# Feature sums of a linear attention: added up in one tile, formed behind the denominators, turned a period later

## The chip, the cores and the metric

The kernel runs on one core of one Trainium2 chip. A core has a matrix engine (TensorE, PE in the profile; its weight loads are PEld), a vector engine (DVE), an activation engine (ACT), a general one (POOL) and a queue that issues DMAs (SP). The metric is the device time of the whole program in microseconds, the median of several runs; less is better.

## The reference

Linear attention over 8 batches and 8 heads of 576 positions, followed by a dense layer pair.

```python
def phi(x):
    proj = np.einsum('bhsd,df->bhsf', x, w_phi)
    proj = proj - np.max(np.abs(proj), axis=-1, keepdims=True)
    return np.concatenate([np.exp(proj), np.exp(-proj)], axis=-1)
q_p, k_p = (phi(q), phi(k))
kv = np.einsum('bhsf,bhsd->bhfd', k_p, v)
z = np.sum(k_p, axis=2)
num = np.einsum('bhsf,bhfd->bhsd', q_p, kv)
den = np.einsum('bhsf,bhf->bhs', q_p, z)[..., None] + 1e-06
attn = num / den            # heads side by side: x, 4608 x 512
h = x @ w_in                # 512 -> 2048
out = (h - np.tanh(h)) @ w_out
```

z are the feature sums: 256 per head (128 features, two signs).

## The kernel before

**Stage one, attention.** A unit is a pair of heads (e = 0, 1) of one batch; there are NU = 32 of them, and u.i is a unit's number. A unit's 576 positions of q and of k make 9 blocks of 128: four and a half of q, four and a half of k. The half block of k is tile j = 0 of five (64 rows, from SR = 64 up), the whole ones are j = 1 to 4.

The work is a pipeline over periods, period(i) for i from 0 to 32, written out by hand: inside manual_schedule every engine's queue follows the order of the program. In period i the unit a = i is projected, c = i - 1 gets its products of k and v and the exponentials of q, p = i - 2 its numerators and denominators, r = i - 3 its reciprocals, and q = i - 4 the multiplication by them and its store. Beside that, a weight block w per period is decoded on DVE from 64-bit numbers (dec_0 on ACT, dec_1 to dec_3 on DVE), and in periods 3 to 16 one is split into a high and a low part (split_w).

PE's order in a period, with the names of its outputs in the profile:

- project(a, 0): pp, three blocks of both heads. DVE then takes the largest magnitude (L223) and subtracts it (less_max, L230) into tile t. The PSUM tile of pp has one buffer, so each project waits for the subtraction of the one before.
- num(p): po, the numerators, from kv and the exponentials qe of q.
- project(a, 1), then kv(c): pc, the products of k's features with v. ACT copies it to kvt (kv_copy, L291).
- project(a, 2).
- ksum(c): pk, the feature sums as products with a column of ones. The full tiles 1 to 4 were added up by POOL before (kadd, L274 to L276: three adds into the tile t of the third projection), so pk takes that sum and then the half tile apart. ACT copies pk to kst (ksum_copy).
- q_side(c): ptr and ptt, transposes of q's blocks; ACT takes their exponentials.
- turn(c): ptk, transposes of the two halves of kvt and of kst; DVE copies them to SBUF (turn_copy, L305).
- denom(p): pd, the denominators; ACT copies them to dd (denom_copy), and SP loads them into another layout (dn, den_recip_load).

A period later DVE takes the reciprocals (rn, L357 and L358), SP sends them through DRAM (rr) to all partitions (rb), and after that POOL multiplies (den_mul, L367) and SP stores the result to xs. All these DMAs stand in the one queue of SP in program order, with the loads of q, k, v and the raw weights.

POOL's helper behind(x) copies one column of a tile (mark, L186), which makes POOL wait until DVE has written it; it stands ahead of POOL's part of split_w (L96) and at a period's end behind the decode.

On PE, one fp32 matmul stands as two records in the profile. A shape such as 128*32 is the rows and columns of the array that a matmul takes: pk with the full tile and pd both have 128*32, pk with the half tile has 64*32, pp and ptr 64*128, ptt and ptk 128*128, po and pc 128*64.

**Stage two, the dense layers.** The result is read back in groups of 384 tokens: x_load brings four column blocks (192 KB each), x_split makes a high part on ACT (L114) and a low one on DVE (L115). The tile x has four buffers. The four blocks of the first group are loaded at the start of period 30 and split at the end of period 31. Stage two (L508 on) then runs 192 steps, a step being one group by one block of 128 hidden features; its order is left to the planner, but for the instructions marked with pin.

What follows the periods (L490 to L496) is also left to the planner: the reciprocals, multiplications and stores of the last three units.

Of the kernel before, what the change touches and what calls it, by code (L numbers as in the profile page):

```python
# [8 lines left out]
F32 = mybir.dt.float32  # L9
# [4 lines left out]
ALU = mybir.AluOpType  # L14
# [5 lines left out]
P = 128  # L20
# [12 lines left out]
def tile_linear_attention_moe(  # L33
# [10 lines left out]
    nc = tc.nc  # L44
    B, H, S, D = dims
    F = w_phi.shape[1]
# [4 lines left out]
    SR = S - SM  # L51
# [4 lines left out]
    G = 3  # L56
    AHEAD = 7
    PC = 2 * S
    NCT = DM // P
# [8 lines left out]
    ident = consts.tile([P, P], F32, name="ident")  # L68
# [10 lines left out]
    xp0 = ctx.enter_context(tc.tile_pool(name="xp0", bufs=1, reuse_waits="tile"))  # L79
# [25 lines left out]

    def x_load(g, xt, c):
        bp, o = divmod(g * G, TPP)
        x = xp0.tile([P, G * P], F32, tag="x", name=f"x{g}_{c}", bufs=4)
        nc.sync.dma_start(x, xs[bp][c, :, o * P : (o + G) * P])
        xt[2][c] = x  # L110

    def x_split(xt, c, order=lambda ins: ins):
        xh, xl, x = xt
        order(nc.scalar.copy(xh[:, c, :], x[c]))  # L114
        order(nc.vector.tensor_tensor(xl[:, c, :], x[c], f32(xh[:, c, :]), ALU.subtract))  # L115
# [5 lines left out]
    with ExitStack() as c1:  # L121
        raw = c1.enter_context(tc.tile_pool(name="raw", bufs=2))
        p1 = c1.enter_context(tc.tile_pool(name="p1", bufs=1))
        p2 = c1.enter_context(tc.tile_pool(name="p2", bufs=2))
# [4 lines left out]
        ps_d = c1.enter_context(tc.tile_pool(name="ps_d", bufs=3, space=PSUM))  # L129
# [55 lines left out]
        def behind(x):  # L185
            nc.gpsimd.tensor_copy(mark, f32(x[:, 0:1]))  # L186
# [64 lines left out]
            for s in range(2):  # L251
                nc.scalar.activation(u.qe[:, :, s, SM:S], x, AF.Exp, scale=1.0 - 2.0 * s)

        def k_exp(u, r):
            x, j0, j1 = (u.t[1][:, :, 1:3, :], 0, 2) if r == 1 else (u.t[2], 2, 5)
            for s in range(2):
                nc.scalar.activation(u.kp[:, :, j0:j1, s, :], x, AF.Exp, scale=1.0 - 2.0 * s)


        KT = (1, 2, 3, 4, 0)  # L260

        def kv(u):
            u.pc = ps_c.tile([P, 512], F32, tag="pc", name=f"pc{u.i}")
            for j in KT:
                r = slice(SR, P) if j == 0 else slice(0, P)
                for e in range(2):
                    nc.tensor.matmul(  # L267
                        u.pc[e * D : (e + 1) * D, 0 : 2 * F], u.v[r, j, e, :], u.kp[r, e, j, :, :], start=(j == KT[0]), stop=(j == KT[-1])
                    )


        def kadd(u):
            x = u.t[2].rearrange("p e a f -> p (e a f)")[:, 0 : 4 * F].rearrange("p (e s f) -> p e s f", e=2, s=2)
            nc.gpsimd.tensor_tensor(x, u.kp[:, :, 2], u.kp[:, :, 3], ALU.add)  # L274
            nc.gpsimd.tensor_tensor(x, x, u.kp[:, :, 4], ALU.add)
            nc.gpsimd.tensor_tensor(x, x, u.kp[:, :, 1], ALU.add)  # L276
            u.ss = x

        def ksum(u):
            u.pk = ps_d.tile([P, 512], F32, tag="po", name=f"pk{u.i}")  # L280
            parts = [(slice(0, P), u.ss)] if u.ss is not None else [(slice(0, P), u.kp[:, :, j]) for j in KT[:-1]]
            parts.append((slice(SR, P), u.kp[:, :, 0]))
            for a, (r, x) in enumerate(parts):
                for n in range(4):
                    nc.tensor.matmul(  # L285
                        u.pk[n * 32 : (n + 1) * 32, 0:F], ones[r, :], x[r, n // 2, n % 2, :], start=(a == 0), stop=(a == len(parts) - 1)
                    )

        def kv_copy(u):
            u.kvt = p1.tile([P, 2, F], F32, tag="kvt", name=f"kvt{u.i}")  # L290
            nc.scalar.copy(u.kvt.rearrange("p a f -> p (a f)"), u.pc[:, 0 : 2 * F])  # L291

        def ksum_copy(u):
            u.kst = p1.tile([P, F], F32, tag="kst", name=f"kst{u.i}")
            nc.scalar.copy(u.kst, u.pk[:, 0:F])


        def turn(u):
            u.pt = ps_d.tile([P, 512], F32, tag="po", name=f"ptk{u.i}")
            for a, x in enumerate([u.kvt[:, 0, :], u.kvt[:, 1, :], u.kst]):  # L300
                nc.tensor.transpose(u.pt[:, a * P : (a + 1) * P], x, ident)  # L301

        def turn_copy(u):
            t = p2.tile([P, 3, P], F32, tag="kv", name=f"kv{u.i}")
            nc.vector.tensor_copy(t.rearrange("p a c -> p (a c)"), u.pt[:, 0 : 3 * P])  # L305
            u.kv, u.ks = t, t[:, 2, :]


        def num(u):
            u.po = [ps_d.tile([P, 512], F32, tag="po", name=f"po{u.i}_{c}") for c in range(2)]  # L310
            for s in range(2):
                for c in range(2):
                    for e in range(2):
                        nc.tensor.matmul(  # L314
                            u.po[c][e * D : (e + 1) * D, 0:CH],
                            u.kv[:, s, e * D : (e + 1) * D],
                            u.qe[:, e, s, c * CH : (c + 1) * CH],
                            start=(s == 0),
                            stop=(s == 1),
                        )  # L320
# [16 lines left out]
        def num_copy(u):  # L337
            u.d = tail.tile([P, S], F32, tag="d", name=f"d{u.i}", bufs=2)
            for c in range(2):
                nc.scalar.copy(u.d[:, c * CH : (c + 1) * CH], u.po[c][:, 0:CH])  # L340
# [5 lines left out]
        def den_recip_load(u):  # L346
            w = 2 * S // P
            dn = tail.tile([P, w], F32, tag="dn", name=f"dn{u.i}")
            nc.sync.dma_start(dn, u.dd.rearrange("(n r) c -> n r c", r=32)[:, 0, :])
            u.dn = dn  # L350
# [22 lines left out]
        for i in range(B * NHP):  # L373
            u = Unit()
# [3 lines left out]
        NU = len(units)  # L378
# [20 lines left out]
        def period(i):  # L399
            a, c, p, r, q = (unit(i - n) for n in range(5))  # L400
            w = dec[i - 2] if 2 <= i < NU + 2 else None
            if q:
                den_mul(q)
                x_store(q)
            if i == NU - 2:
                xt[0] = x_tiles(0)
                for j in range(NCT):
                    x_load(0, xt[0], j)
            if a:
                a.kp = p2.tile([P, 2, 5, 2, F], F32, tag="kp", name=f"kp{i}")  # L410
                if i == 0:
                    warm(16)
                project(a, 0)
                less_max(a, 0)
            if c:
                k_exp(c, 2)
                if i < NU:
                    kadd(c)
            if p:
                num(p)  # L420
                num_copy(p)
            if r:
                den_recip(r)
            low = split_w(i - 3) if 3 <= i <= 2 * AHEAD + 2 else None
            if w:
                dec_0(w)
            if i == 1:
                warm(8)
            if a:
                project(a, 1)  # L430
                less_max(a, 1)
            if i == 1:
                warm(16)
            if c:
                kv(c)
                kv_copy(c)
            if i + 1 < NU:
                load_v(units[i + 1])
            if a:
                k_exp(a, 1)  # L440
            if w:
                dec_1(w)
                if low:
                    behind(w.a)
                    low()
            if a:
                project(a, 2)
            if i + 2 < NU:
                load(units[i + 2])
            if c:  # L450
                ksum(c)
                ksum_copy(c)
            if a:
                less_max(a, 2)
            if c:
                q_side(c)
                turn(c)
            if c:
                turn_copy(c)
            if w:  # L460
                dec_2(w)
                dec_3(w)
            if p:
                denom(p)
                denom_copy(p)
                if i < NU:
                    den_recip_load(p)
            if w:
                behind(w.d[w.f])
                if i < NU:  # L470
                    dec.append(dec_load(i))
            if i == NU:
                num(c)
                num_copy(c)
                w = dec[NU - 1]
                dec_0(w)
                dec_1(w)
                dec_2(w)
                dec_3(w)
                denom(c)  # L480
                denom_copy(c)
            if i == NU - 1:
                for j in range(NCT):
                    x_split(xt[0], j)

        xt = {}
        with tc.manual_schedule():
# [12 lines left out]
    with ExitStack() as c2:  # L500
# [67 lines left out]
        po, gs, gg = {}, {}, {}  # L568
        for i in range(len(steps) + 2):
            if i < len(steps):  # L570
                g, f = steps[i]
# [10 lines left out]
            if 1 <= i <= len(steps):  # L582
                g, f = steps[i - 1]
# [8 lines left out]
            if i >= 2:  # L592
                g, f = steps[i - 2]
# [58 lines left out]
```

## Time and profile before

| | us |
|---|---|
| median of 3 runs | 1181.67 (1179.06 to 1183.47) |
| the profiled execution, whole | 1179.44 |
| its span, first to last instruction | 1177.6 |
| PE busy in the span | 1157.2 (98%) |
| DVE busy | 907.6 (77%) |
| ACT busy | 806.0 (68%) |
| POOL busy | 412.6 (35%) |

The attention periods fill the first 356 us of the span, the dense layers the rest. Where a row of the timeline has several instructions (x8), its length is from the start of the first to the end of the last. In square brackets stand the idle time of the engine ahead of it and what ended that.

### The profile page before, as it was taken

How to read it: one execution, taken by the hardware profiler on the slowest of the kernel's cores; microseconds unless marked ns; L12 is line 12 of the kernel's file. 1: busy time of each engine (PE TensorE's matmuls, PEld its weight loads, DVE VectorE, ACT ScalarE, POOL GpSimd, SP SyncE). 2: the span in 40 equal slices, each digit the busy share in tenths (PEclk: the TensorE clock that was granted, in tenths of full speed). 3: DMA queues.
4: the chain of work that ended last, by engine and by line, in shares of the span. 5: the costliest groups of instructions: out<-in, count | busy, mean ns of one | idle time of the engine just before them, and what ended most of it. 6: DMA issues, size and time to landing. Idle time of an engine off the chain costs nothing.

```text
span 1177.6 us, 21218 instructions
## 1 busy us (share of the span) xinstructions
PE 1157.2 (98%) x7840; PEld 950.1 (81%) x7840; DVE 907.6 (77%) x1464; ACT 806.0 (68%) x1748; POOL 412.6 (35%) x404
## 2 busy tenths in 40 slices
PE   8999999999998999999999999999999999999998
PEld 6666666666656889999999999999999999999996
DVE  6999998989877977777777767777777767777665
ACT  4777776666666767676676667676666767666665
POOL 2566664455435652222222222222222222222222
PEclk9999999999999999999999999999999999999999
DMA  5565565566551000010000001000000001000000
GB/s 165 178 194 190 180 206 183 189 189 209 182 177 61 14 19 30 14 41 15 34 14 34 21 8 41 14 34 21 34 14 35 15 13 41 14 28 1 28 1 28
DMA packets 51177, 85.64 MB, mean 73 GB/s; under 512 B 13312, under 2 KB 28160, under 8 KB 51072
## 3 DMA queue, kind: packets, MB, share of 16 engines
q1 hardware_dynamic: 50912, 84.20, 22.2%
q8 instruction: 62, 1.02, 0.3%
q14 instruction: 43, 0.35, 0.1%
q10 hardware_dynamic: 160, 0.07, 0.0%
HBM read 65.08 MB, written 19.02 MB: 71 GB/s over the span
## 4 chain that ended last, share of the span: by engine, by line
PE 91%; DVE 3%; POOL 2%; DMA 2%; ACT 1%; issue 1%; DVEq 0%; SPq 0%; POOLq 0%; ACTq 0%
PE ph L516 33%; PE po L553 11%; PE po L550 11%; PE po L551 11%; PE pp L214 7%; PE pc L267 6%; PE po L314 5%; PE ptt L236 3%; PE pd L329 3%; PE pk L285 2%; PE ptk L301 1%; DMA rb<-rr 1%; PE ptr L242 1%; DMA dn<-dd 1%; DVE s L537 0%
## 5 line engine op out<-in xcount | busy, mean ns | idle before, releaser
L544 POOL TENSOR_TENSOR gl<-s,gh 128x384 fp32r<-128x384 f32 x192 | 197.9, 1031 | 569.1 <-ACT gh L543 562.8
L516 PE MATMUL ph<-xh,wli 128*128 128x384 f32 x768 | 261.0, 340 | 1.3 <-POOL wli L96 1.3
L516 PE MATMUL ph<-xl,whi 128*128 128x384 f32 x768 | 260.2, 339 | 0.0
L516 PE MATMUL ph<-xh,whi 128*128 128x384 f32 x768 | 259.6, 338 | 0.3 <-DVE th L536 0.3
L523 ACT ACTIVATE y<-ph 128x384 f32<-128x384 f32 x192 | 94.5, 492 | 238.6 <-PE ph L516 238.6
L532 DVE SCALAR_TENSOR_TENSOR s<-s,y 128x384 f32<-128x384 f32 x192 | 107.8, 561 | 168.3 <-ACT s L525 168.2
L550 PE MATMUL po<-who,gh 128*128 128x512 f32 x576 | 227.1, 394 | 1.6 <-ACT gh L543 1.6
L551 PE MATMUL po<-wlo,gh 128*128 128x512 f32 x576 | 226.1, 393 | 0.0
L553 PE MATMUL po<-who,gl 128*128 128x512 f32 x576 | 164.8, 395 | 5.3 <-POOL gl L544 5.3
L537 DVE COPY_PREDICATED s<-mk,th 128x384 f32<-128x384 uint32 x192 | 140.3, 731 | 20.8 <-DVE th L536 1.4
L516 PEld LDWEIGHTS ph<-xh,whi 128*128 128x128 f32 x768 | 146.2, 190 | 9.0 <-DVE th L536 0.6
L516 PEld LDWEIGHTS ph<-xl,whi 128*128 128x128 f32 x768 | 144.6, 188 | 8.2
L516 PEld LDWEIGHTS ph<-xh,wli 128*128 128x128 f32 x768 | 144.9, 189 | 2.0 <-POOL wli L96 1.9
L553 PEld LDWEIGHTS po<-who,gl 128*128 128x128 f32 x576 | 107.9, 188 | 30.8 <-POOL gl L544 6.9
L533 DVE SCALAR_TENSOR_TENSOR s<-s,s 128x384 f32<-128x384 f32 x192 | 115.0, 599 | 20.1 <-ACT mk L531 0.9
L550 PEld LDWEIGHTS po<-who,gh 128*128 128x128 f32 x576 | 109.1, 189 | 20.7 <-ACT gh L543 3.4
L551 PEld LDWEIGHTS po<-wlo,gh 128*128 128x128 f32 x576 | 108.0, 187 | 16.8
L527 ACT ACTIVATE s<-y,bias_t 128x384 f32<-128x384 f32 x192 | 118.0, 615 | 4.9 <-POOL gl L544 4.7
L531 ACT ACTIVATE mk<-y,bias_t 128x384 f32<-128x384 f32 x192 | 117.9, 614 | 2.9 <-DVE s L537 2.9
L525 ACT ACTIVATE s<-y,bias_t 128x384 f32<-128x384 f32 x192 | 118.5, 617 | 0.0
L535 DVE SCALAR_TENSOR_TENSOR s<-s,ph 128x384 f32<-128x384 f32 x192 | 106.2, 553 | 6.3
L214 PEld LDWEIGHTS pp<-wph,qk 64*128 64x128 f32 x1152 | 73.4, 188 | 44.2 <-PE po L314 15.9
(75 smaller groups left out, 1707.8 us busy)
## 6 DMA issues: line engine op xcount, KB each, us to landing
qk<-in_qkT SPq DMA_DIRECT2D x31, 576.0 KB, 4.9
v<-in_v SPq DMA_DIRECT2D x32, 320.0 KB, 4.0
rb<-rr SPq DMA_DIRECT2D x64, 144.0 KB, 3.0
xs<-rb SPq DMA_DIRECT2D x32, 288.0 KB, 3.7
x<-xs SPq DMA_DIRECT2D x48, 192.0 KB, 2.3
out<-o SPq DMA_DIRECT2D x36, 256.0 KB, 2.1
rawi<-in_moe_w_in SPq DMA_DIRECT2D x16, 512.0 KB, 3.9
rawo<-in_moe_w_out SPq DMA_DIRECT2D x16, 512.0 KB, 6.3
```

What stands on the lines that cost most here:

```text
L214: nc.tensor.matmul(pp[e][:, a * F : (a + 1) * F], u.qk[hs, j * P : (j + 1) * P], wph[hs, :], start=True, stop=True)
L516: nc.tensor.matmul(h, wt[:, c * P : (c + 1) * P], x[:, c, 0:N], start=(i == 0), stop=(i == 3 * NCT - 1))
L525: nc.scalar.activation(s1, y, AF.Square, bias=bias_t[:, 0:1])
L527: nc.scalar.activation(s2, y, AF.Square, bias=bias_t[:, 1:2])
L531: nc.scalar.activation(mk, y, AF.Relu, bias=bias_t[:, 2:3])
L532: nc.vector.scalar_tensor_tensor(s1, s1, PC1, y, ALU.add, ALU.mult)
L533: nc.vector.scalar_tensor_tensor(s2, s2, PC2, s1, ALU.add, ALU.mult)
L537: nc.vector.copy_predicated(gs, mk.bitcast(U32), th)
L544: pin(nc.gpsimd.tensor_tensor(gl, gs, f32(gh), ALU.subtract))
L550: nc.tensor.matmul(po[t], a, wo[f][0], start=(f == 0), stop=False)
L551: nc.tensor.matmul(po[t], a, wo[f][1], start=False, stop=False)
L553: nc.tensor.matmul(po[t], gl[:, t * P : (t + 1) * P], wo[f][0], start=False, stop=(f == NF - 1))
```

## The change

ksum(c) moves from the middle of the period to its end, behind denom(p), and reads one tile. POOL adds four terms instead of three: kadd makes the sum of the tiles 1 to 4 in a tile of its own (ss, no longer in t), and kadd_rest adds the half tile into its upper 64 rows, behind a mark on the decode of the period. kadd is left out in the first period that has a unit c, where pk then takes the five tiles.

The sums of unit c are copied to kst at the start of the next period (when that unit is p) and turned there, together with the kvt of the next unit: turn and turn_copy stand ahead of q_side now, and turn_copy ahead of the third subtraction (less_max(a, 2)). The turned tile kv has one buffer of four blocks; denom(p) reads block 2 of the tile that was turned in the same period. The last unit's sums are turned by themselves (turn_last).

k_exp(a, 1) is cut in two; the first sign now stands ahead of kv_copy on ACT. The tile x has two buffers instead of four: two blocks of the first group are loaded in period 30 and split in period 32, where the other two are loaded and, at the end, split.

```diff
@@ -105,7 +105,7 @@
 
     def x_load(g, xt, c):
         bp, o = divmod(g * G, TPP)
-        x = xp0.tile([P, G * P], F32, tag="x", name=f"x{g}_{c}", bufs=4)
+        x = xp0.tile([P, G * P], F32, tag="x", name=f"x{g}_{c}", bufs=2)
         nc.sync.dma_start(x, xs[bp][c, :, o * P : (o + G) * P])
         xt[2][c] = x
 
@@ -251,9 +251,9 @@
             for s in range(2):
                 nc.scalar.activation(u.qe[:, :, s, SM:S], x, AF.Exp, scale=1.0 - 2.0 * s)
 
-        def k_exp(u, r):
+        def k_exp(u, r, signs=(0, 1)):
             x, j0, j1 = (u.t[1][:, :, 1:3, :], 0, 2) if r == 1 else (u.t[2], 2, 5)
-            for s in range(2):
+            for s in signs:
                 nc.scalar.activation(u.kp[:, :, j0:j1, s, :], x, AF.Exp, scale=1.0 - 2.0 * s)
 
 
@@ -270,16 +270,21 @@
 
 
         def kadd(u):
-            x = u.t[2].rearrange("p e a f -> p (e a f)")[:, 0 : 4 * F].rearrange("p (e s f) -> p e s f", e=2, s=2)
+            x = p1.tile([P, 2, 2, F], F32, tag="ss", name=f"ss{u.i}")
             nc.gpsimd.tensor_tensor(x, u.kp[:, :, 2], u.kp[:, :, 3], ALU.add)
             nc.gpsimd.tensor_tensor(x, x, u.kp[:, :, 4], ALU.add)
             nc.gpsimd.tensor_tensor(x, x, u.kp[:, :, 1], ALU.add)
             u.ss = x
 
+        def kadd_rest(u):
+            nc.gpsimd.tensor_tensor(u.ss[SR:P], u.ss[SR:P], u.kp[SR:P, :, 0], ALU.add)
+
         def ksum(u):
             u.pk = ps_d.tile([P, 512], F32, tag="po", name=f"pk{u.i}")
-            parts = [(slice(0, P), u.ss)] if u.ss is not None else [(slice(0, P), u.kp[:, :, j]) for j in KT[:-1]]
-            parts.append((slice(SR, P), u.kp[:, :, 0]))
+            if u.ss is not None:
+                parts = [(slice(0, P), u.ss)]
+            else:
+                parts = [(slice(0, P) if j else slice(SR, P), u.kp[:, :, j]) for j in KT]
             for a, (r, x) in enumerate(parts):
                 for n in range(4):
                     nc.tensor.matmul(
@@ -291,19 +296,28 @@
             nc.scalar.copy(u.kvt.rearrange("p a f -> p (a f)"), u.pc[:, 0 : 2 * F])
 
         def ksum_copy(u):
-            u.kst = p1.tile([P, F], F32, tag="kst", name=f"kst{u.i}")
+            u.kst = p2.tile([P, F], F32, tag="kst", name=f"kst{u.i}")
             nc.scalar.copy(u.kst, u.pk[:, 0:F])
 
 
-        def turn(u):
-            u.pt = ps_d.tile([P, 512], F32, tag="po", name=f"ptk{u.i}")
-            for a, x in enumerate([u.kvt[:, 0, :], u.kvt[:, 1, :], u.kst]):
-                nc.tensor.transpose(u.pt[:, a * P : (a + 1) * P], x, ident)
-
-        def turn_copy(u):
-            t = p2.tile([P, 3, P], F32, tag="kv", name=f"kv{u.i}")
-            nc.vector.tensor_copy(t.rearrange("p a c -> p (a c)"), u.pt[:, 0 : 3 * P])
-            u.kv, u.ks = t, t[:, 2, :]
+        def turn(c, p):
+            c.pt = ps_d.tile([P, 512], F32, tag="po", name=f"ptk{c.i}")
+            c.turned = [c.kvt[:, 0, :], c.kvt[:, 1, :]] + ([p.kst] if p else [])
+            for a, x in enumerate(c.turned):
+                nc.tensor.transpose(c.pt[:, a * P : (a + 1) * P], x, ident)
+
+        def turn_copy(c, p):
+            n = len(c.turned)
+            c.kv = p1.tile([P, 4, P], F32, tag="kv", name=f"kv{c.i}")
+            nc.vector.tensor_copy(c.kv[:, 0:n, :].rearrange("p a c -> p (a c)"), c.pt[:, 0 : n * P])
+            if p:
+                p.ks = c.kv[:, 2, :]
+
+        def turn_last(c):
+            pt = ps_d.tile([P, 512], F32, tag="po", name="ptl")
+            nc.tensor.transpose(pt[:, 0:P], c.kst, ident)
+            nc.vector.tensor_copy(c.kv[:, 3, :], pt[:, 0:P])
+            c.ks = c.kv[:, 3, :]
 
 
         def num(u):
@@ -404,7 +418,7 @@
                 x_store(q)
             if i == NU - 2:
                 xt[0] = x_tiles(0)
-                for j in range(NCT):
+                for j in range(2):
                     x_load(0, xt[0], j)
             if a:
                 a.kp = p2.tile([P, 2, 5, 2, F], F32, tag="kp", name=f"kp{i}")
@@ -414,11 +428,17 @@
                 less_max(a, 0)
             if c:
                 k_exp(c, 2)
-                if i < NU:
+                if 1 < i < NU:
                     kadd(c)
             if p:
+                ksum_copy(p)
                 num(p)
                 num_copy(p)
+            if i == NU:
+                for j in range(2):
+                    x_split(xt[0], j)
+                for j in range(2, NCT):
+                    x_load(0, xt[0], j)
             if r:
                 den_recip(r)
             low = split_w(i - 3) if 3 <= i <= 2 * AHEAD + 2 else None
@@ -433,30 +453,37 @@
                 warm(16)
             if c:
                 kv(c)
+            if a:
+                k_exp(a, 1, (0,))
+            if c:
                 kv_copy(c)
             if i + 1 < NU:
                 load_v(units[i + 1])
             if a:
-                k_exp(a, 1)
+                k_exp(a, 1, (1,))
             if w:
                 dec_1(w)
-                if low:
-                    behind(w.a)
-                    low()
+            if c and c.ss is not None:
+                behind(w.a)
+                kadd_rest(c)
+            if low:
+                low()
             if a:
                 project(a, 2)
             if i + 2 < NU:
                 load(units[i + 2])
-            if c:
+            if i == NU:
                 ksum(c)
                 ksum_copy(c)
+            if c:
+                turn(c, p)
+                turn_copy(c, p)
             if a:
                 less_max(a, 2)
             if c:
                 q_side(c)
-                turn(c)
-            if c:
-                turn_copy(c)
+            if i == NU:
+                turn_last(c)
             if w:
                 dec_2(w)
                 dec_3(w)
@@ -465,11 +492,15 @@
                 denom_copy(p)
                 if i < NU:
                     den_recip_load(p)
+            if c and i < NU:
+                ksum(c)
             if w:
                 behind(w.d[w.f])
                 if i < NU:
                     dec.append(dec_load(i))
             if i == NU:
+                for j in range(2, NCT):
+                    x_split(xt[0], j)
                 num(c)
                 num_copy(c)
                 w = dec[NU - 1]
@@ -479,9 +510,6 @@
                 dec_3(w)
                 denom(c)
                 denom_copy(c)
-            if i == NU - 1:
-                for j in range(NCT):
-                    x_split(xt[0], j)
 
         xt = {}
         with tc.manual_schedule():
```

## The prediction

> **What bounds the kernel now.** I read the head of the page first, then the table of windows, then the chain of waits through one period.
>
> ```profile
> span 1177.6 us, 21218 instructions
> 200.00:220.00 20.00, 19.89 (x222) 12.48 (x221) 18.34 (x24) 13.22 (x30) 10.13 (x10) 1.00 0.63 204
> 360.00:380.00 20.00, 15.18 (x73) 12.65 (x72) 18.18 (x28) 14.65 (x32) 11.59 (x9) 1.00 0.22 71
> ```
>
> The columns after the window's length are PE, PEld, DVE, ACT and POOL. In the attention periods PE is busy for 19.89 of 20 us, DVE for 18.34. Behind the change of stages (360 to 380) PE idles for nearly 5 us. The chain of waits, start and length in us, shows one period:
>
> ```profile
> 242.01 0.87 PE pp L214 x12
> 242.88 0.71 PE pk L285 x16
> 243.58 0.27 PE ptr L242 x2
> 243.85 1.02 PE ptt L236 x8
> 244.87 0.33 PE ptk L301 x3
> 245.20 1.11 PE pd L329 x16
> 246.31 0.87 PE pp L214 x12
> 247.18 2.12 PE po L314 x16
> 249.29 0.03 issue
> 249.32 0.94 PE pp L214 x12
> 250.26 2.46 PE pc L267 x20
> ```
>
> No other engine is in it: from pp at 242.01 to the end of pc at 250.26 + 2.46 = 252.72 is one period, 10.71 us, all PE. So a steady period is worth what its PE queue takes, as long as the other engines keep up. I number the three projections of a period pp0, pp1, pp2; the one at 242.01 is pp2.
>
> **The change, part by part: PE.** Only the stretch from pp2 to the next pp0 is reordered: before pk, ptr, ptt, ptk, pd; after ptk, ptr, ptt, pd, pk. Its price is read from the starts of the weight loads, in the timeline of PEld:
>
> ```profile
> 242.80 0.16 PEld L285 LDWEIGHTS pk<-t,ones 128*32 128x32 f32 x8
> 243.16 0.15 PEld L285 LDWEIGHTS pk<-kp,ones 64*32 64x32 f32 x8 [0.20 <-issue]
> 243.51 0.20 PEld L242 LDWEIGHTS ptr<-ident,t 64*128 64x128 f32 x2 [0.20 <-issue]
> 243.78 0.86 PEld L236 LDWEIGHTS ptt<-ident,t 128*128 128x128 f32 x8
> 244.60 0.25 PEld L301 LDWEIGHTS ptk<-ident,kvt 128*128 128x128 f32 x2
> 244.82 0.14 PEld L301 LDWEIGHTS ptk<-ident,kst 128*128 128x128 f32 x1
> 245.13 0.64 PEld L329 LDWEIGHTS pd<-qe,kv 128*32 128x32 f32 x16 [0.17 <-PE ptk L301]
> 246.24 0.75 PEld L214 LDWEIGHTS pp<-wph,qk 64*128 64x128 f32 x12 [0.47 <-DVE kv L305]
> ```
>
> - The eight records of the half tile (kp, 64 rows) go: 243.51 - 243.16 = -0.35.
> - The eight records of the full tile take 243.16 - 242.80 = 0.36 now, 0.20 of it the pause before the next shape. Behind pd, which has the same shape 128*32, they need no pause of their own. pd spends 246.24 - 245.13 = 1.11 on 16 records of 288 columns; by columns, 8 records of 128 are (8 x 128)/(16 x 288) = 0.22 of that, 0.25. So -0.11. The ends are 0.16 (their weight loads alone) and 0.36 (a block with its own pause).
> - ptk used to stand behind ptt in one shape: eight ptt in 244.60 - 243.78 = 0.82, so three are worth about 0.31. Alone between two other shapes, a run of three with its exit takes 245.13 - 244.60 = 0.53. ptt then pays the exit that ptk paid. So +0.53 - 0.31 - 0.05 for the change between pp2 and pk's shape that both have = about +0.17; ends 0.10 and 0.25.
>
> Sum per period: -0.35 - 0.11 + 0.17 = **-0.29 us**, a period of 10.42; from the ends -0.10 to -0.45.
>
> The Trainium skill ("TensorEngine Tiling (Array Packing)", Key Properties) says that a change of tiling mode, not of tile, drains the engine. By it alone the count of changes matters: pk, pk of 64 rows, ptr, ptt, pd, pp are six, and ptk, ptr, ptt, pd, pp five, one pause of 0.20 less; with the records that go, that lies inside the range above. It speaks against the new place of ptk and for that of pk.
>
> **What the other engines must now hold.** DVE's timeline in the same stretch:
>
> ```profile
> 242.92 0.96 DVE L223 TENSOR_REDUCE m<-pp 128x6 f32<-128x768 f32 x1 [0.19 <-PE pp L214]
> 244.01 0.96 DVE L230 TENSOR_TENSOR t<-pp,m 128x768 f32<-128x768 f32 x1
> 245.24 0.56 DVE L305 COPY kv<-ptk 128x384 f32<-128x384 f32 x1 [0.27 <-PE ptk L301]
> 245.71 0.68 DVE L175 SCALAR_TENSOR_TENSOR dec_ai<-rawi,dec_ai 128x512 uint32<-128x512 uint32 x1
> 246.43 0.69 DVE L179 SCALAR_TENSOR_TENSOR wi<-rawi,dec_ai 128x512 uint32<-128x512 uint32 x1
> ```
>
> The new wait: denom needs the feature sums from turn_copy, which now stands between the reduce and the subtraction (L230). ptk ends at about 243.4, so turn_copy starts when the reduce is done, 243.88, and ends at 244.44. PE wants to start pd at 242.80 + 0.53 + 0.27 + 1.03 = 244.63. **0.19 us are spare**. Behind a late pd stand pk, pp0 and all of PE. The subtraction then ends near 245.4, L175 near 246.1, L179 near 246.75; the reduce of pp0 is due at 246.92 (4.31 behind pp2's start, less 0.29). Spare 0.17. pp0 to pp2 is unchanged on PE and DVE. I cost DVE at nothing; if it runs late by more than these, PE pays each further tenth.
>
> ACT and POOL:
>
> ```profile
> 242.11 0.37 ACT L291 COPY kvt<-pc 128x256 f32<-128x256 f32 x1 [2.53 <-PE pc L267]
> L367 POOL TENSOR_TENSOR rb<-d,rb 128x576 f32<-128x576 f32 x22 | 31.2, 1417 | 0.1
> 102.88 1.28 POOL L96 TENSOR_TENSOR wli<-wi,whi 128x512 fp32r<-128x512 f32 x1
> 107.10 0.19 POOL L186 COPY mark<-wo 128x1 f32<-128x1 f32 x1 [2.95 <-DVE wo L179]
> L561 DVE COPY o<-po x24: 680/684/692, 439.1 to 1173.2; 128x512 f32<-128x512 f32 x24
> DMA to landing us min/median/max: 2.4/3.7/4.7
> ```
>
> The half of k_exp moved ahead of kv_copy falls into ACT's 2.53 us of idle time; kvt then ends about 0.05 later, 0.25 ahead of the turn. ksum_copy moves to where ACT waits for num; it lengthens nothing on PE.
>
> POOL gains a fourth add: as wide as L96 (512 columns) on half the partitions, so 1.28, and a mark, 0.19, in the periods that had none. Ahead of the marks at a period's end POOL idles for 2.95 us even in the periods that also split weights (L96), so it fits: it ends where L96 ends now, 104.16, and pk reads the sums about 2.3 us later, where pd now ends less 0.29 and pk's own 0.25. In those 14 periods L96 now runs 1.28 later and ends at 102.88 + 2 x 1.28 = 105.44, 0.4 behind the start of L175 (about 105.0, by the period above moved to this one); L175 then ends up to 0.15 later, within DVE's 0.17. I take +0.5 us in all, ends 0 and 2.
>
> The Trainium skill ("SBUF — State Buffer", Who interferes with whom) speaks against the added POOL work: a DVE instruction with two SBUF inputs, or in a two-port mode, and a GpSimd one that reads SBUF block each other for a whole instruction, while one with at most one SBUF input does not contend. The trace agrees where it can: copies from PSUM (L561) stay within 680 to 692 ns whatever POOL does, and so the turn_copy, the reduce and the subtraction beside the fourth add should be safe.
>
> DMA: the ring dn, rr, rb starts at the same place behind pp0 and is used one period later, so it loses 0.29. An rb lands up to 4.7 us after its issue. In the 22 steady periods the multiplication that reads it (L367) idles for 0.1 in all, so 0.29 less will make a few periods' POOL late by 0.1 to 0.3, which DVE's spare takes for the most part: +0.3, ends 0 and 3.
>
> Period 1 has no adds now: pk takes five tiles there, about 1 us more, but the wait for POOL in it goes. I take 0 (ends -0.5 and +0.7). The new tiles ss, kst and kv each have their last reader done before the next writer: 0.
>
> **The change of stages.** Before:
>
> ```profile
> 343.13 0.41 ACT L344 COPY dd<-pd 128x288 f32<-128x288 f32 x1
> 343.42 1.75 ACT L114 CAST xh<-x 128x384 fp32r<-128x384 f32 x4
> 346.70 2.10 PE L267 MATMUL pc<-kp,v 128*64 128x256 f32 x16 [1.17 <-ACT kp L257]
> 347.52 0.32 SPq L359 DMA_DIRECT2D rr<-rn  x1
> 355.02 1.42 POOL L367 TENSOR_TENSOR rb<-d,rb 128x576 f32<-128x576 f32 x1 [9.21 <-DMA rb<-rr]
> 356.84 2.98 SPq L349 DMA_DIRECT2D dn<-dd  x2
> 358.82 0.40 ACT L344 COPY dd<-pd 128x288 f32<-128x288 f32 x1 [1.09 <-DMA dn<-dd]
> ```
>
> The four x_split at the end of period 31 hold ACT for 1.75 us and so kv for 1.17. That stall goes, but it is not worth 1.17: the chain runs dd (343.13), dn, rn, rr (347.52), rb, the multiplication at 355.02, its store, the next dn (356.84, behind it in SP's queue), dd at 358.82, and only then do ACT's stage-1 instructions follow. So what is late next is rb. In the new order dd of period 31 comes 0.4 earlier (pd earlier by 0.4), but rn stands behind two splits that wait for num_copy, and rr behind two x loads in SP's queue: about 347.7 to 348.0 against 347.52. The rb behind it meets two x loads of 192 KB, not three. I take -0.5, ends -3 (SP gets past the store, dn early) and +2 (rb late by the x loads). The later two x_split fit before stage 1. Two x buffers in the second stage: a load waits for the split two before it, six steps ahead of its use, 0.
>
> **Sum.** Periods 2 to 31: 30 x -0.29 = -8.7; +0.5 +0.3 -0.5 makes -8.4. The profiled execution took 1179.44 (span 1177.6 and 1.84 around it): 1171.0. The median of the three runs is 1181.67, 2.2 above it, which would give 1173.3. I put the prediction between, **1172**. Within 0.5% is within 5.9 us of 1181.67, about what a measurement of this kernel can tell from no change.
>
> **Rivals.**
> - **A wait in place of the wait.** turn_copy comes late by 0.3 to 0.5 beyond its spare 0.19 and PE idles ahead of pd; the gain goes. For it: DVE has 0.19 and 0.17 spare. Against: its durations are steady. 1179 (no change), chance 0.08.
> - **Little of the gain.** pk keeps a pause of its own (0.36, not 0.25) and ptk costs 0.25, the dear ends: -0.10 a period, -3; with the late rb and the early pinch nearly nothing is left of it: 1177 to 1180. Chance 0.11.
> - **The change of stages.** rb late by the x loads: +2, not -0.5, 1174.5 (chance 0.07); SP past the store: -3, 1169.5, and less if POOL's waits behind it shrink too (0.10).
> - **Slower.** POOL doesn't get through before DVE's decode: its adds slip by the fourth's 1.28 and hold the decode (L171, L172) that stands ahead of the reduce, and so turn_copy and pd. It decides when the decode ends later than now by the reduce's idle 0.19 and turn_copy's spare 0.19; then PE pays 1.28 - 0.38 = 0.90 and keeps 0.29, +0.61 a period. In the 14 periods with L96 alone that is +8.5 on them and -4.6 on the others, no change that can be told; in all 30, +18: 1199. Against it are the 2.95 us of idle POOL; for it, that rb can be late. Chance 0.08.
> - **It doesn't do what it says:** the fourth add is late and pk waits for it at the period's end. It has 2.3 us spare; 0.03, at 1180.
>
> **The numbers.** The forecast itself, 1169 to 1175.5, has 0.53; with the change of stages to both sides 0.70 lies below 1175.8. Faster 0.70; same 0.08 + 0.11 + 0.03 = 0.22; slower 0.08. For 8 in 10 the range takes in the lost gain (1179) at the top and the better change of stages with a cheap ptk below: 1166 to 1179.5.
>
> **What would show it.** In the chain of waits of a steady period: ptk 0.5, pd and pk together 1.3 to 1.4, 10.4 from pp2 to pp2, and no piece but PE. Right before pd no PE idle time released by DVE's turn_copy. L175 at 0.68 late in the loop, longer while weights are split. No 1.17 stall of pc in period 32, rr at 348 less the periods' gain, and PE's idle time behind the change of stages about as large as before. A DVE or POOL piece in the steady chain would make the prediction wrong.

## The result, and the profile after

Six runs of the changed kernel have a median of 1172.29 us (1169.13 to 1176.76), six of the kernel before beside them 1179.69 (1177.56 to 1183.47). The ratio is 0.994, with a 95% interval of 0.9921 to 0.9958: faster by some 0.6%. The forecast was 1172.0. The profiled execution of the changed kernel is the slowest of its six (1176.76, span 1175.0); what it lost against the others is the main finding below.

The head of the page after, and the chain of waits by engine:

```profile
span 1175.0 us, 20830 instructions
PE 86%; DVE 7%; DMA 3%; ACT 1%; issue 1%; POOL 1%; SPq 0%; DVEq 0%; POOLq 0%; ACTq 0%
```

The same line of the kernel before:

```profile
PE 91%; DVE 3%; POOL 2%; DMA 2%; ACT 1%; issue 1%; DVEq 0%; SPq 0%; POOLq 0%; ACTq 0%
```

PE's share has fallen from 91% to 86%, and DVE's has grown from 3% to 7%. Two kinds of period stand behind that in the chain of waits. First an undisturbed one (start, length, what):

```profile
220.70 0.87 PE pp L214 x12
221.57 0.48 PE ptk L307 x3
222.05 0.26 PE ptr L242 x2
222.31 1.02 PE ptt L236 x8
223.34 1.11 PE pd L343 x16
224.44 0.22 PE pk L290 x8
224.66 0.87 PE pp L214 x12
225.53 2.11 PE po L328 x16
227.65 0.03 issue
227.68 0.94 PE pp L214 x12
228.61 2.46 PE pc L267 x20
```

From 220.70 to 228.61 + 2.46 = 231.07 it is 10.37 us, all PE, against 10.71 before. From ptk to the end of pk it is 3.09, where the stretch from pk to pd took 3.44. A period later the same view leaves PE:

```profile
234.39 0.98 ACT qe L247 x2
235.37 0.30 ACT dd L358
235.69 3.36 DMA dn<-dd
...
239.14 0.93 DVE rn L371
...
240.31 0.82 DVE m L223
...
241.15 0.97 DVE t L230
...
242.26 0.94 PE pp L214 x12
```

dn, the 4.5 KB of denominators, lands 3.36 us after its issue. DVE's reciprocal waits for it ahead of the second reduce, the subtraction ends late, and PE's third projection waits for that. The waits of 60 to 300 us (engine, line, cause: us in total, times, longest) show the cause and not the sufferer:

```profile
DVE rn L371 <- DMA dn<-dd: 9.6, 9, 1.8
POOL rb L381 <- DMA rb<-rr: 1.1, 3, 0.7
```

The distances between the starts of pc, taken from PE's timeline, account for most of the difference of the spans. The kernel before has 29 of 30 within 10.70 to 10.76 and one of 11.67. The changed one has 10.30 to 10.38 where nothing disturbs it (once 10.55) and 10.52 to 10.54 where weights are split. Seven are longer (11.53, 10.76, 11.49, 11.49, 13.04, 11.28, 11.16): 8.2 us over 10.37. In six of the seven DVE's reciprocal waits for dn, and PE's third projection then waits 0.70 to 1.08; ahead of the seventh (10.76) it had waited too, 0.94, and PE waits 0.45 at its second projection. The 30 distances sum to 322.2 before and 320.1 after, where 30 x 10.37 would be 311.

### The profile page after: what moved, and what is told of

Its sections match the earlier page's. It is cut to its first block, busy times and chain, and to the rows that moved or that the text cites. A ratio compares the mean times of both kernels' runs of the same rounds, so it can differ in the third digit from the quotient of the medians.

```text
span 1175.0 us, 20830 instructions
## 1 busy us (share of the span) xinstructions
PE 1149.6 (98%) x7624; PEld 949.1 (81%) x7624; DVE 898.8 (76%) x1465; ACT 804.7 (68%) x1748; POOL 449.9 (38%) x447
## 4 chain that ended last, share of the span: by engine, by line
PE 86%; DVE 7%; DMA 3%; ACT 1%; issue 1%; POOL 1%; SPq 0%; DVEq 0%; POOLq 0%; ACTq 0%
PE ph L544 33%; PE po L578 11%; PE po L581 11%; PE po L579 11%; PE pp L214 6%; PE pc L267 5%; PE po L328 3%; PE ptt L236 2%; PE pd L343 2%; DMA dn<-dd 2%; DVE t L230 2%; DVE m L223 2%; PE ptk L307 1%; DVE rn L371 1%; DMA qk<-in_qkT 1%
## 5 line engine op out<-in xcount | busy, mean ns | idle before, releaser
L257 ACT ACTIVATE kp<-t 128x768 f32<-128x768 f32 (+1 forms) x128 | 92.0, 754 | 72.0 <-DVE t L230 72.0
L223 DVE TENSOR_REDUCE m<-pp 128x6 f32<-128x768 f32 (+1 forms) x99 | 91.1, 922 | 27.0 <-PE pp L214 26.1
```

What stands on the lines that cost most here:

```text
L223: nc.vector.tensor_reduce(m[:, e], x, AX.X, ALU.max, apply_absolute_value=True)
```

## The experiments

Times are medians where there were rounds, and one execution where there were none; the kernel before ran beside each on the same chip, at 1179.7 to 1181.2. "Distance" is always that between the starts of pc.

**1. q and k behind dn.** In a disturbed period the queue of SP looks otherwise than in an undisturbed one. Rows of SP's timeline, first behind rr at 217.73 (no wait for dn), then behind rr at 228.45 (1.24 us of wait):

```profile
220.41 1.10 SPq L376 DMA_DIRECT2D rb<-rr  x2
221.61 0.53 SPq L199 DMA_DIRECT2D v<-in_v  x1
222.24 0.38 SPq L195 DMA_DIRECT2D qk<-in_qkT  x1
225.32 0.59 SPq L363 DMA_DIRECT2D dn<-dd  x1
...
231.36 1.10 SPq L376 DMA_DIRECT2D rb<-rr  x2
232.56 0.53 SPq L199 DMA_DIRECT2D v<-in_v  x1
233.19 0.38 SPq L195 DMA_DIRECT2D qk<-in_qkT  x1
235.69 0.59 SPq L363 DMA_DIRECT2D dn<-dd  x1
```

qk is issued 3.1 us ahead of dn in the one, 2.5 in the other: rr comes 0.35 later in its period, and rb waits 0.23 longer for it. Over the loop, the eleven waits for dn stand where qk was issued 1.2 to 2.5 us ahead of dn. Where it was 2.7 or more there is none, but at 1.9 to 2.2 three dn came in time, so this distance is not all. So q and k were put behind dn:

```diff
-            if i + 2 < NU:            # behind project(a, 2)
-                load(units[i + 2])
...
                 if i < NU:
                     den_recip_load(p)
+            if i + 2 < NU:
+                load(units[i + 2])
             if c and i < NU:
                 ksum(c)
```

> The changed kernel with one edit: in each period the load of the next q and k (576 KB) is issued behind the small load dn of the denominators instead of ahead of it. Theory A (the gain that is missing is lost to dn, 4.5 KB, which lands behind the 896 KB of v, q and k issued 1.2 to 3 us before it; where SP got past rr late it lands 3 to 4 us after its issue instead of 2.1, DVE waits for it ahead of the second reduce and PE behind DVE): dn lands within about 2.2 to 2.5 us in every period, DVE's waits for dn (9.6 us in 60 to 300 in the changed kernel) fall under 2, nearly all periods are 10.36 to 10.54, and the whole is 4 to 6 us faster than the changed kernel, about 1167. Rival B (dn is slow by itself, as a chain of small descriptors, or by the traffic of the raw weights): the waits stay, time as the changed kernel, 1172. Rival C: q and k now delay rr and rb by as much, POOL starts late and stretches DVE's decode: POOL waits for rb appear, no gain or a loss.

It took 1190.33, ratio 1.0095 (1.0077 to 1.0112): slower than before. The waits over 60 to 300 us are

```profile
POOL rb L381 <- DMA rb<-rr: 15.8, 13, 2.7
DVE rn L371 <- DMA dn<-dd: 6.8, 10, 1.6
```

rb is issued only when rr has landed, and between the two issues lay 3.3 to 6.0 us now, where it was 1.4 to 4.0. Rival C had it right, and theory A was too narrow: with the bulk ahead of rr it is rr that comes late, and dn still does in ten periods.

**2. dn in a queue of its own.** `nc.sync.dma_start(dn, ...)` became `nc.scalar.dma_start(dn, ...)`.

> The changed kernel with dn issued from ACT's DMA queue, right behind the copy dd on ACT, everything else as it is. If dn is late because it stands in one queue with v, q and k (Theory A, in order in the queue's rings), a queue of its own lands it in about 2.1 us and the time falls as with q and k behind it, to about 1167 to 1169 (ACT pays up to 0.6 us per issue, which its idle time of 3 us ahead of the fourth exponential takes). If it is late because the 16 engines are busy with the 896 KB whatever the queue, the waits stay and the time is as the changed kernel's, 1172.

It took 1196.82, ratio 1.0137 (1.0113 to 1.0162). The timelines of SP, ACT and DVE show what dn met:

```profile
231.72 0.38 SPq L155 DMA_DIRECT2D rawi<-in_moe_w_in  x1
...
231.77 0.53 ACTq L363 DMA_DIRECT2D dn<-dd  x1
...
235.59 1.07 DVE L371 TENSOR_SCALAR rn<-dn 128x9 f32<-128x9 f32 x1 [1.62 <-DMA dn<-dd]
```

SP no longer holds the raw weights (512 KB) back behind dn, so they start with it, and dn takes 3.8 us. The edit thus changed the bulk that stands beside dn too, and this run doesn't tell what a queue of its own is worth. It does tell that such a queue doesn't shield dn. The Trainium skill ("Trainium Kernel Development and Optimization", Key Constraints) says that DMAs from different issuing engines run on the same 16 DMA engines and interleave; this trace agrees, with the 3.8 us of dn in ACT's queue beside SP's bulk.

**3. The half tile apart.** pk at its new place, without POOL's fourth add:

```diff
-                parts = [(slice(0, P), u.ss)]
+                parts = [(slice(0, P), u.ss), (slice(SR, P), u.kp[:, :, 0])]
...
-            if c and c.ss is not None:
-                behind(w.a)
-                kadd_rest(c)
             if low:
+                behind(w.a)
                 low()
```

> The changed kernel without POOL's fourth add: pk reads the sum of four tiles and then the half tile apart, at the period's end. The steady period of the changed kernel is 10.36, of the one before 10.71. Theory: of the 0.35 nearly all is the half tile's eight records with their pause, and the moves of ptk and pk cancel: an undisturbed period of 10.70 to 10.75, with the 0.15 that the periods with split weights lose (10.52) gone. Rival: the moves bring a good part of the gain by themselves: an undisturbed period of 10.45 to 10.6.

Undisturbed distances are 10.71 to 10.76, with and without split weights, and the time of its one execution was 1177.83. In its chain pd and pk are

```profile
255.74 1.11 PE pd L343 x16
256.85 0.57 PE pk L290 x16
```

against 1.11 and 0.22 above. So the half tile is the whole gain on PE (0.35), and the moves of pk and ptk cancel. Only two of 30 distances are disturbed (11.45 and 11.13), so the new order alone doesn't bring the many late dn. This run lacks the fourth add as well as the shorter period; it doesn't tell these two apart.

**4. The x part alone,** on the kernel before (two buffers, splits and loads where the change has them).

> The kernel before with only the x part of the change: two buffers, two blocks split in period 32 behind the numerators, the other two loaded there and split at the end. The first y of stage two stands 14.18 us behind the start of the last pc in the kernel before and 13.45 in the changed one. Theory: the move is worth that 0.7 by itself (13.3 to 13.6), because dn of unit 30 gets past the store of unit 29 in SP's queue; the time is 0 to 1 us below the kernel before. Rival: it is the earlier dd of period 31, from the attention part, that brings it, and alone the move is worth nothing or a loss (14.2 or more).

From the start of the last pc (345.18) to the first y of stage two (358.36) it is 13.18, against 14.18 before, and the time of its one execution was 1177.85. In SP's queue the dn of unit 30 now stands ahead of the store:

```profile
353.08 0.58 SPq L349 DMA_DIRECT2D dn<-dd  x1
...
356.93 0.32 SPq L370 DMA_DIRECT2D xs<-rb  x1
```

So the x part by itself shortens the stretch, by some tenths up to 1.0. The size is uncertain: these are single traces, the stretch is 12.82 to 13.45 in the changed kernel and its variants up to experiment 7 and in 11, and in experiment 10, which keeps the old x part, it is 13.49.

**5. Without the loads of q and k.** `load(units[i + 2])` became `units[i + 2].qk = a.qk`, so the kernel leaves out 576 KB of loads in each period.

> The changed kernel without the loads of q and k behind the second unit (every later unit computes on the first two units' q and k): 576 KB less per period in SP's queue, all else in place. With q and k behind dn the time rose to 1190, since rr then landed 3.3 to 5.9 us after its issue instead of 1.4 to 3.9; so the theory is now that the ring dn, rn, rr, rb, multiplication has to close once per period, that each of its small transfers lands late by the bulk issued just ahead of it, and that the shorter period has taken its slack. Then, without the bulk ahead of dn, dn lands in 2.1 to 2.3 in every period, the waits for it are gone, periods are 10.36, and 10.52 where weights are split, and the span is about 1175.0 less the 8 us of disturbed periods in that profile: 1166 to 1168. Rival (dn is late by itself, for instance by its own descriptors, or by DVE or ACT): periods of 11 and more stay, 1172.

It took 1168.47, ratio 0.9887 (0.9869 to 0.9906). The wait for dn in 60 to 300 us:

```profile
DVE rn L371 <- DMA dn<-dd: 0.3, 1, 0.3
```

Distances are 10.30 to 10.37 and 10.51 to 10.55, but for one of 11.28. That is about what the changed kernel is without late transfers; it loses 3.8 us of it by the medians, some 6 by the ratios to the kernel before beside each. The rival of a dn that is late by itself falls. Whether the place of q and k in the queue counts or their traffic is not told apart, as both are gone.

The one long distance has another cause. DVE's decode (L172) takes 1.38 there beside POOL's third add where it takes 0.43 in other periods, turn_copy is late, and pd waits:

```profile
113.75 1.18 PE L343 MATMUL pd<-qe,kv 128*32 128x288 f32 x16 [0.40 <-DVE kv L312]
```

**6. v, q and k between rr and rb.** The loads moved half a period on, into den_recip between the store of rr and the loads of rb.

> The changed kernel with the loads of v and of q and k issued between rr and rb, half a period later, so that neither dn nor rr has them just ahead; rb has. By the theory of the ring dn lands in 2.1 to 2.5 and the waits for it go; rb is issued at its old place or earlier behind 896 KB and lands up to 2 us later, and POOL's multiplication, which had nothing to spare, waits for it. If rb's lateness stays under about 0.4 the time is 1167 to 1169; if it is over 1 us, POOL's adds slip and the time is as the changed kernel's or worse (1172 to 1185). Rival (the bulk's place does not matter): time and waits as in the changed kernel.

It took 1176.69, ratio 0.9956 (0.9938 to 0.9974). No reciprocal waits for dn in 60 to 300 us. But the distances scatter from 10.34 to 11.53, since rb lands late (POOL's multiplication waits for it seven times, 3.1 us in all) and q and k themselves do:

```profile
PE pp L214 <- DMA qk<-in_qkT: 3.7, 9, 0.7
```

**7. The reciprocals behind the second subtraction.** den_recip(r) moved behind less_max(a, 1), nothing else.

> The changed kernel with the reciprocals (rn) behind the second subtraction on DVE instead of ahead of the second reduce: a late dn no longer holds the reduce, but rr and rb go out about 2 us later. Theory of the ring: it is only moved on, the multiplication on POOL waits for rb by 1 to 2.5 us in every period, its adds slip and DVE's decode with them: 1180 to 1200. Rival (only the place of rn in DVE's queue costs, the ring has slack elsewhere): 1166 to 1168.

It took 1184.06 in its one execution. The wait is where the theory of the ring put it, though in 14 periods with 0.8 on the average and not in every one with 1 to 2.5, in

```profile
POOL rb L381 <- DMA rb<-rr: 11.1, 14, 2.5
```

**8. The same, and the multiplication a period later.**

```diff
-            a, c, p, r, q = (unit(i - n) for n in range(5))
+            a, c, p, r, _, q = (unit(i - n) for n in range(6))
...
-            u.d = tail.tile([P, S], F32, tag="d", name=f"d{u.i}", bufs=2)
+            u.d = tail.tile([P, S], F32, tag="d", name=f"d{u.i}", bufs=3)
```

> As the one with rn behind the second subtraction, and the multiplication and its store one period later (unit i - 5 instead of i - 4, d in three buffers; kst in one, and the last unit's turned sums in kvt, to find the room): the ring then has a whole period more for rb and 2 us more for dn. Theory of the ring: no wait for dn or rb in the loop, periods of 10.36 and 10.52, the change of stages within 1 us of the changed kernel's: 1164 to 1168, faster than both. Rival (period bound by PE and DVE with disturbances that don't come from the ring): 1172.

It took 1171.88, ratio 0.9917 (0.9899 to 0.9936). From 185 us on, distances are 10.36 to 10.37 with one of 10.77, behind the only dn that came late (0.89): the ring has nearly all its slack. The forecast of 1164 to 1168 missed the periods with split weights, which are 10.80 to 10.82. There rn, behind the second subtraction, puts off the decode and the third reduce, and PE waits half a microsecond for the next subtraction.

**9. Both later, rn at its old place.** r is unit i - 4 and q unit i - 5.

> The changed kernel with the reciprocals at their old place in the period but of the unit before (i - 4 instead of i - 3), and the multiplication and the store of unit i - 5; d in three buffers, kst in one, the last unit's turned sums in kvt. dn then has a whole period more; rb has what it has in the changed kernel. In the one with rn behind the second subtraction the late periods were 10.37, but those with split weights 10.81, as rn and its stretch by POOL's adds stood ahead of the decode there; in the changed kernel those are 10.52. Theory of the ring: no wait for dn, 10.37 late and 10.52 with split weights, save where a late rb holds POOL (1.1 us of such waits in the changed kernel); the time as without the loads of q and k, 1167 to 1169, 12 below the kernel before and 3 to 4 below the one with rn later. Rival (the ring closes just as late, since rr and rb still follow the bulk): periods of 11 and more come back through rb, 1172.

It took 1169.95, ratio 0.9917 (0.9900 to 0.9935). No reciprocal inside the loop waits for dn, the undisturbed distances are 10.30 to 10.37 and 10.52 to 10.55, and four are 10.64 to 10.91. What is left is in part in rb, as the rival had it, only smaller:

```profile
POOL rb L381 <- DMA rb<-rr: 3.8, 5, 1.5
```

Two of the four (10.91 and 10.64) follow the longest waits for rb, 1.5 and 1.3, with pd waiting 0.47 and 0.20 for turn_copy. The median is 1 us above the forecast, and the lead over experiment 8 isn't there by the ratio (0.9917 in both). It is 2.3 below the changed kernel's median, but the two intervals of the ratio overlap (0.9921 to 0.9935), so that lead is likely, not shown. That it is faster than the kernel before is shown.

**10. The fourth add alone,** on the kernel before, with pk at its old place on one tile.

> The kernel before with only the fourth add on POOL, at the changed kernel's place behind the mark on the decode; pk at its old place, on one tile. Theory: POOL has the sum at about 244.3 of the period shown, where pk is due at 242.8, so PE waits about 1.4 for POOL and saves 0.35: an undisturbed period of 11.6 to 11.9, 1205 to 1220. It would say that the moves of pk and of the turn, worth nothing by themselves, are what makes the 0.35 reachable. Rival: PE's queue or the later subtraction hides most of the wait and the period stays within 0.2 of 10.7.

It took 1223.87 in its one execution, above the forecast. Distances are 11.5 to 12.0 but for the first (12.83) and six of 13.4 to 13.6. These seven have a fall of PE's granted clock in them (see the last section). PE's timeline:

```profile
247.66 0.43 PE L289 MATMUL pk<-t,ones 128*32 128x128 f32 x8 [1.20 <-POOL t L280]
```

The add that is worth 0.35 costs a wait of 1.1 to 1.6 where pk stood. So the moves, worth nothing by themselves on PE, are what makes it usable.

**11. The exponential whole.** k_exp(a, 1) with both signs behind kv_copy, as before the change.

> The changed kernel with both signs of the first exponential of k behind kv_copy again, as before the change. Theory: the split is worth nothing on PE: kvt is ready 0.2 to 0.3 before the turn either way, and the second exponential ends before ptr's are due or 0.2 behind; undisturbed periods stay 10.36 to 10.40 (10.52 with split weights), the time within the scatter of the changed kernel. Rival: the exponentials of q start late, dd and with it dn go out 0.3 to 0.5 later, and more periods wait for dn: 1174 to 1178.

It took 1171.89, with distances of 10.29 to 10.37 and 10.53 to 10.55, three of 10.43 to 10.62 and five of 11.1 to 11.3. The split can't be told from nothing in one run.

## Why the prediction was right, and what in it was not

**PE, -0.29 a period: right in kind, a little small.** Undisturbed periods lost 0.34. The half tile's 0.35 was right, and experiment 3 shows it: with the half tile back, the period is the old one. pk behind pd came to 0.22 (0.25 predicted), the run of ptk to 0.48 where 0.53 was taken.

**DVE's spare: right, and as small as said.** In undisturbed periods the chain is PE alone, as the prediction's sign had it, and PE doesn't idle ahead of pd. pd's weight loads do wait for turn_copy, 18 times in 60 to 300 us, by up to 0.2. The rivals of a wait in place of the wait, of little gain, and of POOL holding the decode did not come in the changed kernel. They can be near: in experiments 5, 8 and 9 pd waits 0.20 to 0.47 for turn_copy in one or two periods, in experiment 7 up to 1.6, and in experiment 10 a late POOL holds PE in each.

**The pinch with split weights: the mechanism right, the size at the dear end.** Rows of POOL and DVE in the changed kernel:

```profile
168.45 1.29 POOL L96 TENSOR_TENSOR wli<-wi,whi 128x512 fp32r<-128x512 f32 x1
...
169.01 1.28 DVE L175 SCALAR_TENSOR_TENSOR dec_ao<-rawo,dec_ao 128x512 uint32<-128x512 uint32 x1
```

L175 takes 1.28, not 0.68, and the distance is 10.52, not 10.37. In experiment 5 eleven distances show it, 0.14 to 0.18 each: near the 2 us that were the dear end, where +0.5 was taken. The term went wrong in L175: it was to end up to 0.15 later, and beside L96 it took 0.60 more. The third reduce and turn_copy beside the fourth add kept their 0.96 and 0.55. The Trainium skill ("SBUF — State Buffer", Who interferes with whom) says that a DVE instruction with at most one SBUF input, outside the two-port modes, does not contend with GpSimd; this trace agrees, as both read PSUM.

**The step that failed: "the ring dn, rr, rb ... +0.3, ends 0 and 3".** The ring was named, but its price was read off the one place that showed idle time before, the multiplication's wait for rb. The place that broke first is dn, ahead of the second reduce; in the profiled execution it and the clock behind it cost most of 8 us, and in the median 3.8 or more by experiment 5. The kernel before already had eight waits for dn in the loop (0 to 350 us):

```profile
DVE rn L357 <- DMA dn<-dd: 4.6, 8, 1.0
```

All but one were covered by DVE's spare; behind the longest, PE waited 0.90. So the ring had less slack than the single row for rb told.

**The change of stages: right.** -0.5 was predicted; from the last pc to the first y it is 13.45 after against 14.18. The way was the one given as the cheap end, at a far smaller size than its 3 us: SP got past the store with dn of unit 30, in experiment 4 as well.

```profile
350.64 0.59 SPq L363 DMA_DIRECT2D dn<-dd  x1
...
354.78 0.32 SPq L384 DMA_DIRECT2D xs<-rb  x1
...
355.96 0.39 ACT L358 COPY dd<-pd 128x288 f32<-128x288 f32 x1
356.23 0.50 ACT L551 ACTIVATE y<-ph 128x384 f32<-128x384 f32 x1
```

The dd of the last unit no longer waits for a dn (1.09 before); what is left ahead of it is rb and its multiplication, as predicted.

**The sum: close in part by luck.** 1172.0 against 1172.29 is better than its terms. With the sizes found (PE -10.2, the pinch +1.8, late transfers +3.8, the change of stages -0.7) they give -5.3 from 1179.69, so some 1174.4. PE gave 1.5 more than predicted, the pinch and the late transfers took that and some 3 us more. That the median is 2 us below this sum no run explains; the runs of the changed kernel spread over 1169.13 to 1176.76.

## What to carry to other kernels

When the engine that bounds a loop is made faster, every ring (a chain of dependent steps that must close once per turn) loses the same time, here 0.34 us. List the rings, dependent DMAs above all, and read the spare of each link, not only of the one with the most visible wait. Here a load of 4.5 KB was there within 2.1 to 2.5 us in the periods without a wait, and took some 3 to 4 in the others, where bulk was issued shortly ahead of it. Moving the bulk moved the lateness to the next small transfer, and a period more between issue and use took nearly all the waits for dn away (experiments 8 and 9); that it also makes the whole faster than the changed kernel is not shown. An edit that gains nothing by itself (the moves of pk and ptk) may be what lets another be used.

## What the hardware showed that was not expected

The longest of the disturbed distances, 13.04, is not explained by its wait alone. PE waited 0.95 us ahead of the third projection, and then its clock fell:

```profile
208.62 0.94 PE L214 MATMUL pp<-wph,qk 64*128 64x128 f32 x12 [0.95 <-DVE t L230]
```

Rows of the table of windows (length, busy times, then the granted clock, DMA share and GB/s):

```profile
204.00:208.00 4.00, 3.62 (x34) 2.03 (x32) 2.17 (x5) 1.22 (x3) 3.58 (x3) 1.00 0.64 207
208.00:212.00 4.00, 3.38 (x25) 2.81 (x25) 3.64 (x7) 2.50 (x7) 1.45 (x2) 0.79 0.52 161
212.00:216.00 4.00, 4.00 (x45) 2.26 (x46) 1.96 (x3) 3.23 (x7) 1.55 (x2) 0.78 0.42 147
```

In the chain ptt takes 1.85 there instead of 1.02 and pd 1.90 instead of 1.11, 1.6 us more. The Trainium skill ("TensorE: Matmul & The Clock Gate", Why this matters for your kernels) advises no idle gaps over about 3 us to keep the clock; here gaps of 0.95 us and less came ahead of the fall, and the measurement decides. Other waits of about 1 us in the same run (1.08, 1.03 and 1.02) cost no clock.

Such falls are not the change's own. The kernel before has one in stage two (0.76 and 0.81 granted from 424 to 432 us), experiment 2 has five before stage two and experiment 10 seven. In experiment 2 ten waits of PE last 1.34 to 1.37 us, and the clock falls behind two of them. So the length of a wait doesn't decide it alone, and what does stays open. The times show the falls too: of the 13 executions of the kernel before beside experiments 5 to 8, the six with a mean granted clock of 0.993 to 0.995 took 1180.65 to 1185.89, the seven with 0.997 or 0.998 took 1179.49 to 1181.80.
